# Weight splitting shared with GpSimd, the second token half first, and a new order of the stages

## The chip, the core and the metric

The program runs on one core of a Trainium2 chip, in one launch. The metric is the device time of that launch in microseconds (us): the median of three runs of the kernel before is 595.39 us (595.06 to 596.19). The profiled execution took 595.32 us, of which the span from the first to the last instruction in the trace is 593.5 us.

The engines are named as in the profile: PE is TensorE (its weight loads are PEld), DVE is VectorE, ACT is ScalarE, POOL is GpSimd, SP starts the transfers.

## What is computed

Two stages follow each other for each of 8 batches. The first is attention with 8 heads of 64 columns: 512 local tokens see a window of 32 tokens to each side and 32 global tokens; the 32 global tokens see all. The second is a gated layer over the 544 tokens of the batch.

```
s_l = softmax(0.125 * [q_l k_g^T, q_l k_l^T masked to |i-j| <= 32]);   out_l = s_l [v_g, v_l]
s_g = softmax(0.125 * q_g [k_g, k_l]^T);                               out_g = s_g [v_g, v_l]
x   = concat(out_g, out_l) as [batch, 544, 512]
h   = max(x @ w_in, 0)                       # 512 -> 1024
gate = sigmoid(conv_w[0]*h[t-1] + conv_w[1]*h[t] + conv_w[2]*h[t+1])
out = (h * gate) @ w_out                     # 1024 -> 512
```

The weights (w_in, w_out, conv_w) arrive as 64 bit floating point numbers, handed over as pairs of 32 bit words, and everything else as 32 bit. Both large products are made from two rounded parts of each operand: high times high, high times low, low times high. So each weight has to be turned from its two words into a high part (w0 below) and a low part before the first product that needs it.

## The kernel before

**Tiling.** A batch's attention goes by pairs of heads; a pair takes one load of queries and keys (`qk`), one of values (`vf`), 32 small score products into two banks (`ps_s`, key S), the softmax of each head (DVE finds the maximum and adds the mask, key M, line 285; ACT takes the exponential, key E, line 295), four transposes a head (`ps_t`, T), a copy (`a`, A), 32 small products with the values (`ps_v`, P), a division (`n`, N) and four transposes back (`pv`, U). Its result is rounded into `xh` (ACT) and the rest into `xl` (DVE, line 364), in two halves of the tokens, which overlap by two. The global tokens go by groups of four heads (keys G, GM, GE, GT, GC, GP, GO, GQ, GX), and end in the first 32 columns of the first half.

The gated layer goes by half batches of 272 tokens, `hh` = 0 to 15, and by eighths of the 1024 columns, so that `u` = 8 hh + ft counts 128 units. A unit is 12 products into one bank (`ps_h`, key PZ, line 460), a rectification (ACT, RE), the three taps (C1, Ca, Cb), and by pairs of units a tanh (ACT), the product with h (DVE, GG, line 498), its rounding (ACT, GH) and the rest (GL, line 215). Then come 4 output groups of 24 products (`ps_o`, keys Oa and Ob of 12 each, line 523), a copy (OE) and a store.

**The weights.** w_in and w_out come in four eighths each of 128 x 1024 numbers (index i = 0 to 3 for w_in, 4 to 7 for w_out). For each: a load of 1 MB (WD), the magnitude of the upper word (WA, ACT, line 112), clamp, shift and sign (WC, three DVE operations, lines 119, 120, 123), rounding to the high part (WH, ACT, line 212), and the low part (WL, four DVE operations, lines 126, 130, 132, 134). There is one buffer `wt` for it (`SLOTS["wt"]` = 1), so the next WA waits until the last reader of `wt` is done. Unit u needs eighth ft // 2 of w_in, and output group mt needs eighth 4 + mt.

**The order.** Nothing is left to a scheduler at run time. `plan` lists every step with its engine, an estimated duration (`cost`), what it waits for and a position, `arranged` plays this list through, taking on each engine the ready step with the lowest position, and `emit` writes the instructions in the order that comes out and ties each engine to it. So the tables `POS0` (first batch), `POS` (later batches), `LATE` and `WPOS` (the weights) decide which step stands in front of which on each engine, and each engine runs strictly in that order. `SHARED` names the DVE steps that the planner does not let run beside a POOL step.

In the first batch (`ENG0`) POOL does C1 and GL; in the later ones (`ENG`) C1 alone.

Of the kernel before, what the change touches and what calls it, by code (L numbers as in the profile page):

```python
# [52 lines left out]
def attn_moe(ctx: ExitStack, tc: tile.TileContext, qk_d, vw_d, qg_d, w_in_d, w_out_d, cw_d, out_d):  # L53
# [61 lines left out]

    def scaled_bits(w1, t, keep):

        v = nc.vector
        v.tensor_scalar(out=f(t), in0=f(t), scalar1=LEAST, scalar2=MOST, op0=ALU.max, op1=ALU.min)
        v.tensor_scalar(  # L120
            out=t, in0=t, scalar1=3, scalar2=0x3F800000 | keep, op0=ALU.logical_shift_left, op1=ALU.bitwise_and
        )
        v.scalar_tensor_tensor(out=t, in0=w1, scalar=0xC0000000, in1=t, op0=ALU.bitwise_and, op1=ALU.bitwise_or)  # L123
# [4 lines left out]
    def rest(on, out, w0, w1, p, low):  # L128

        nc.vector.tensor_scalar(out=w1, in0=w1, scalar1=low, scalar2=None, op0=ALU.bitwise_and)  # L130
# [1 line left out]
        v.scalar_tensor_tensor(out=f(w1), in0=w0, scalar=2.0**-32, in1=w1, op0=ALU.mult, op1=ALU.add)  # L132
        if on == "v":
            v.scalar_tensor_tensor(out=out, in0=f(w1), scalar=2.0**-20, in1=f(p), op0=ALU.mult, op1=ALU.mult)
# [61 lines left out]
    def WL(i):  # L196
# [3 lines left out]
        else:  # L200
# [720 lines left out]
```

## Time and profile before

| What | Value |
|---|---|
| median of 3 runs | 595.39 us |
| profiled execution, and its span | 595.32 us, 593.5 us |
| PE busy | 560.9 us, 95% of the span |
| DVE, ACT, POOL busy | 424.0, 324.2, 101.1 us (71%, 55%, 17%) |
| mean granted clock of TensorE | 0.982 |
| chain of work that ended last | PE 84%, DVE 9%, ACT 2% |
| output products (line 523) | 1536, mean 290 ns |
| hidden products (line 460) | 1024 + 512, mean 298 and 292 ns |
| the tap on POOL (line 248) | 128, mean 629 ns |
| the low part on POOL (line 215) | 8, mean 1484 ns |

Busy shares are means over the whole span; the 40 slices of the page and the windows of the trace show where an engine is full. The matmuls overlap each other, so a row's mean is longer than the step from one to the next: 12 of them take 1.52 us in the chain.

### The profile page before, as it was taken

Reading aid. Unit: us, or ns where it says so; the run is one execution under the profiler, and the core shown is the slowest. Engines: PE = TensorE matmul, PEld = TensorE weight load, DVE = VectorE, ACT = ScalarE, POOL = GpSimd, SP = SyncE. Lnnn points to the kernel's source line nnn. Section 1 sums busy time; section 2 is a strip of 40 time slices with the busy share of each in tenths; the row PEclk is TensorE's granted clock in tenths of the full one; section 3 lists DMA queues with packets and bytes.
Section 4 is the critical chain, followed back from the end, with each engine's and each line's share of the span. In section 5 each row is a group of like instructions: output and inputs, shape, how many; then the busy total and the mean of one; then the engine's idle time right before and its main releaser. Section 6 shows DMA issues by size and latency. Waiting matters only on the chain.

```text
span 593.5 us, 20757 instructions
## 1 busy us (share of the span) xinstructions
PE 560.9 (95%) x8704; PEld 528.8 (89%) x8704; DVE 424.0 (71%) x1388; ACT 324.2 (55%) x994; POOL 101.1 (17%) x190
## 2 busy tenths in 40 slices
PE   5656997999999999999999999999999999999997
PEld 3345896999999999999999999999999999999997
DVE  4999999689477948577685858668584856565651
ACT  4954794676477666446565655555565543333320
POOL 6000242033012111121111012111101212221210
PEclk9977999899999999999999999999999999999999
DMA  6987334156234332123333222232412000000001
GB/s 254 390 286 313 95 118 170 39 204 223 91 135 153 107 134 98 56 110 108 135 108 145 100 78 94 100 144 97 146 63 75 20 22 20 29 20 29 30 29 47
DMA packets 22125, 68.46 MB, mean 115 GB/s; under 512 B 2576, under 2 KB 12816, under 8 KB 21008
## 3 DMA queue, kind: packets, MB, share of 16 engines
q1 hardware_dynamic: 22032, 67.14, 31.2%
q8 instruction: 68, 1.11, 0.8%
q14 instruction: 25, 0.20, 0.1%
HBM read 58.22 MB, written 8.91 MB: 113 GB/s over the span
## 4 chain that ended last, share of the span: by engine, by line
PE 84%; DVE 9%; ACT 2%; issue 1%; DMA 1%; POOL 0%; DVEq 0%
PE ps_o L523 32%; PE ps_h L460 31%; PE ps_v L325 5%; PE ps_s L264 4%; PE ps_t L304 4%; PE pv L341 2%; PE psg L278 2%; PE go L422 2%; PE gt L406 1%; DVE pr L285 1%; DVE t L484 1%; DMA vf<-vw 1%; DVE wt L123 1%; DVE raw L132 1%; ACT pr L295 1%
## 5 line engine op out<-in xcount | busy, mean ns | idle before, releaser
L460 PE MATMUL ps_h<-xh,w_in 128*128 128x274 f32 x1024 | 225.4, 298 | 2.8 <-DVE raw L132 1.3
L523 PE MATMUL ps_o<-g,w_out 128*128 128x272 f32 x1536 | 212.2, 290 | 0.0
L523 PEld LDWEIGHTS ps_o<-g,w_out 128*128 128x128 f32 x1536 | 200.0, 189 | 0.2
L460 PEld LDWEIGHTS ps_h<-xh,w_in 128*128 128x128 f32 x1024 | 171.9, 191 | 6.3 <-ACT g L212 1.4
L248 POOL TENSOR_SCALAR t<-hb,cw 128x272 f32<-128x272 f32 x128 | 79.9, 629 | 425.7 <-ACT hb L469 159.2
L460 PE MATMUL ps_h<-xl,w_in 128*128 128x274 f32 x512 | 149.5, 292 | 0.8 <-issue 0.8
L484 DVE SCALAR_TENSOR_TENSOR t<-hb,cw,t 128x272 f32<-128x272 f32 x256 | 125.7, 514 | 30.5 <-POOL t L248 29.1
L295 ACT ACTIVATE pr<-pr,negm 128x128 f32<-128x128 f32 x256 | 99.5, 391 | 47.7 <-DVE negm L285 47.7
L469 ACT ACTIVATE hb<-ps_h 128x273 f32<-128x273 f32 x128 | 50.8, 398 | 93.4 <-PE ps_h L460 91.9
L460 PEld LDWEIGHTS ps_h<-xl,w_in 128*128 128x128 f32 x512 | 98.1, 192 | 1.0 <-issue 1.0
L285 DVE CUSTOM_DVE_ANT_0 pr<-ps_s,mask 128x128 f32<-128x128 f32 x256 | 57.8, 285 | 25.6 <-PE ps_s L264 23.2
L212 DVE COPY o<-ps_o 128x272 f32<-128x272 f32 x64 | 28.0, 438 | 54.8 <-PE ps_o L523 54.6
L212 ACT CAST g<-t 128x544 fp32r<-128x544 f32 x64 | 40.9, 646 | 34.5 <-DVE t L498 22.6
L498 DVE SCALAR_TENSOR_TENSOR t<-t,hb 128x544 f32<-128x544 f32 x64 | 46.0, 719 | 14.3 <-ACT t L493 13.3
L493 ACT ACTIVATE t<-t 128x544 f32<-128x544 f32 x64 | 42.4, 663 | 15.0 <-DVE t L484 13.9
L212 ACT COPY a<-ps_t 128x512 f32<-128x512 f32 x64 | 37.0, 583 | 23.2 <-PE ps_t L304 23.0
L295 ACT ACTIVATION_READ_ACCUMULATOR pr<-pr,negm 128x1 f32 x256 | 48.3, 189 | 0.0
L264 PE MATMUL ps_s<-qk 64*32 64x128 f32 x2048 | 38.4, 283 | 8.4 <-DMA qk<-qk 5.8
L304 PE MATMUL ps_t<-ident,pr 128*128 128x128 f32 x256 | 43.0, 282 | 3.5 <-ACT pr L295 2.5
L215 DVE TENSOR_TENSOR g<-t,g 128x544 fp32r<-128x544 f32 x56 | 41.0, 737 | 6.8 <-ACT g L212 5.3
L264 PEld LDWEIGHTS ps_s<-qk 64*32 64x32 f32 x2048 | 29.9, 109 | 12.7 <-DMA qk<-qk 5.8
L304 PEld LDWEIGHTS ps_t<-ident,pr 128*128 128x128 f32 x256 | 31.1, 144 | 8.2 <-ACT pr L295 7.6
(70 smaller groups left out, 466.1 us busy)
## 6 DMA issues: line engine op xcount, KB each, us to landing
vf<-vw SPq DMA_DIRECT2D x32, 896.0 KB, 6.3
qk<-qk SPq DMA_DIRECT2D x32, 592.0 KB, 4.9
out<-o SPq DMA_DIRECT2D x64, 136.0 KB, 1.7
raw<-w_in SPq DMA_DIRECT2D x4, 1024.0 KB, 6.6
raw<-w_out SPq DMA_DIRECT2D x4, 1024.0 KB, 6.6
qgf<-qg SPq DMA_DIRECT2D x16, 64.0 KB, 2.0
cwr<-cw SPq DMA_DIRECT2D x1, 24.0 KB, 1.9
```

Of the source, the lines that this page charges most:

```text
L212: nc.scalar.copy(out=out, in_=in_) if choice(key) == "a" else eng(key).tensor_copy(out=out, in_=in_)
L248: nc.gpsimd.tensor_scalar(out=out, in0=in_, scalar1=by, scalar2=0.0, op0=ALU.mult, op1=ALU.add)
L264: nc.tensor.matmul(heads[n + j]["s"][b * SG : (b + 1) * SG, t, :], lhsT=qk[rows, i * SG : (i + 1) * SG], rhs=qk[rows, a : a + P], start=Tr ...
L285: nc.vector.tensor_tensor_reduce(out=pr[:, t, :], in0=st["s"][:, t, :], in1=mask[:, t].rearrange("p a c -> p (a c)"), op0=ALU.add, op1=ALU ...
L295: nc.scalar.activation(out=st["p"][:, t, :], in_=st["p"][:, t, :], func=AF.Exp, scale=-1.0, bias=st["m"][:, t : t + 1], accum_out=two["r"] ...
L304: nc.tensor.transpose(out=st["t"][:, t, :], in_=st["p"][:, t, :], identity=ident)
L460: nc.tensor.matmul(ps, lhsT=w[:, ft, ct, :], rhs=x, start=i == 0, stop=i == 3 * NCT - 1)
L469: nc.scalar.activation(out=o, in_=z, func=AF.Relu, scale=0.5)
L484: nc.vector.scalar_tensor_tensor(out=st["t"], in0=st["h"][:, k : k + HALF], scalar=cw[:, 3 * ft + k : 3 * ft + k + 1], in1=st["t"], op0=AL ...
L493: nc.scalar.activation(out=t, in_=t, func=AF.Tanh)
L498: nc.vector.scalar_tensor_tensor(out=t, in0=t, scalar=1.0, in1=h, op0=ALU.add, op1=ALU.mult)
L523: nc.tensor.matmul(ps, lhsT=w[:, mt, ft, :], rhs=g[:, ft, :], start=ft + i == 0, stop=ft == NFT - 1 and i == 2)
```

## The change

- For each eighth of the weights the clamp (a step of its own now, WM, line 117) goes from DVE to POOL. DVE keeps shift and sign (WC, lines 122 and 125).
- The low part is made in another way. WC keeps more bits in `wt`. WL is two DVE operations that do not need the high part: the power of two of the number (line 128) and its product with the lower word (line 214). Two new steps on POOL take the difference of `wt` and the high part (WS, line 221) and add that product (WT, line 226). WT is what the products now wait for. `wt` comes free after WS.
- `TURN` = 1: of each batch the second half of the tokens goes through the gated layer first, so that the first units no longer wait for the global tokens.
- In the first batch C1 goes from POOL to ACT.
- 17 instead of 13 pairs of x buffers; all tables of positions, and some of the planner's durations, are new. `SHARED` loses Ca, Cb, GG, GL and WL.

How many products PE does, and their shapes, stay as they were, 1536 for `ps_h` and 1536 for `ps_o` among them.

The order of the instructions shows three places.

**DVE at the start.** First the kernel before, from the end of the tap weights on: `pr,negm` is M (with a row for its second instruction), `ps_s` the scores.

```order
L132 SCALAR_TENSOR_TENSOR cwr<-cwr 128x24
L134 SCALAR_TENSOR_TENSOR cwp<-cwr,cwp 128x24
L159 TENSOR_TENSOR cw<-cw,cwp 128x24
L285 ISA pr,negm<-ps_s,mask 128x128
L285 ISA negm 128x1
```

Then the change at the same place, with what each waits for:

```order
L135 SCALAR_TENSOR_TENSOR cwp<-cwr,cwp 128x24 [waits DVE_49]
L158 TENSOR_TENSOR cw<-cw,cwp 128x24 [waits DVE_49]
L122 TENSOR_SCALAR wt<-wt 128x1024 [waits Pool_49]
L125 SCALAR_TENSOR_TENSOR wt<-raw,wt 128x1024 [waits DMAHW1_49,DVE_49]
L308 ISA pr,negm<-ps_s,mask 128x128 [waits PE_49]
L308 ISA negm 128x1
```

The first M of the program now stands behind WC of the first eighth, which waits for POOL.

**POOL after its masks.** `wt`, `raw` and `w_in` are the weights, `g` and `t` GL of the first batch. The kernel before has only C1 and GL here; the change has

```order
L117 TENSOR_SCALAR wt<-wt 128x1024
L221 TENSOR_TENSOR w_in_152<-wt,w_in_151 128x1024
L226 TENSOR_TENSOR w_in_152<-w_in_152,raw 128x1024
L117 TENSOR_SCALAR wt<-wt 128x1024
L238 TENSOR_TENSOR g_1169<-t,g_1168 128x544 x2
L221 TENSOR_TENSOR w_out_154<-wt,w_out_153 128x1024
L226 TENSOR_TENSOR w_out_154<-w_out_154,raw 128x1024
L238 TENSOR_TENSOR g_1169<-t,g_1168 128x544
```

the first three rows once for each of four eighths of w_in, then the four of w_out with four GL in between; the other four GL come behind the last eighth.

**SP at the start.** `qk` are queries and keys, `raw` the weights. Before:

```order
L149 DMA cwr<-cw 128x48
L242 DMA qgf<-qg 128x128 x2
L229 DMA qk<-qk 128x1184 x2
L174 DMA raw<-w_in 128x2048
L229 DMA qk<-qk 128x1184
```

and with the change:

```order
L147 DMA cwr<-cw 128x48
L173 DMA raw<-w_in 128x2048
L265 DMA qgf<-qg 128x128 x2
L252 DMA qk<-qk 128x1184 x3
L173 DMA raw<-w_in 128x2048 x2
```

The first eighth of the weights is loaded in front of the first queries and keys.

The core of the diff:

```diff
+    def clamp(e, t):
+        e.tensor_scalar(out=f(t), in0=f(t), scalar1=LEAST, scalar2=MOST, op0=ALU.max, op1=ALU.min)
+
     def scaled_bits(w1, t, keep):
         v = nc.vector
-        v.tensor_scalar(out=f(t), in0=f(t), scalar1=LEAST, scalar2=MOST, op0=ALU.max, op1=ALU.min)
         v.tensor_scalar(
             out=t, in0=t, scalar1=3, scalar2=0x3F800000 | keep, op0=ALU.logical_shift_left, op1=ALU.bitwise_and
         )
...
+    def WM(i):
+        if wpe == 2:
+            clamp(nc.gpsimd, wf[i])
+
     def WC(i):
         if wpe == 2:
-            scaled_bits(raw[i][:, :, 1], wf[i], 0x7FF000)
+            if WAY[i] != "q":
+                clamp(nc.vector, wf[i])
+            scaled_bits(raw[i][:, :, 1], wf[i], 0x7FF000 if WAY[i] == "v" else 0x7FFFF8)
...
-        else:
+        elif WAY[i] == "v":
             p = wf[i]
             power(p, p)
-            rest(choice("WL"), lo, raw[i][:, :, 0], raw[i][:, :, 1], p, 0x1FF)
+            rest(lo, raw[i][:, :, 0], raw[i][:, :, 1], p, 0x1FF)
+        else:
+            w0, p = raw[i][:, :, 0], raw[i][:, :, 1]
+            power(p, wf[i])
+            nc.vector.scalar_tensor_tensor(
+                out=f(w0), in0=w0, scalar=2.0**-52, in1=f(p), op0=ALU.mult, op1=ALU.mult
+            )
+
+    def WS(i):
+        hi, lo = parts(i)
+        if wpe == 2:
+            nc.gpsimd.tensor_tensor(out=lo, in0=f(wf[i]), in1=f(hi), op=ALU.subtract)
+
+    def WX(i):
+        hi, lo = parts(i)
+        if wpe == 2:
+            nc.gpsimd.tensor_tensor(out=lo, in0=f(lo), in1=f(raw[i][:, :, 0]), op=ALU.add)
...
+    def half_of(hh):
+        return (hh + TURN) % 2
+
     def Z(u):
         hh, ft = divmod(u, NFT)
-        b, half = divmod(hh, 2)
+        b, half = hh // 2, half_of(hh)
...
 SLOTS = dict(
-    ps=8, x=13, hb=2, qk=3, vf=3, qg=2, p=4, r=3, a=4, n=2, pg=1, pgt=1, t=2, o=2, wt=1, g0=2, g1=2,
+    ps=8, x=17, hb=2, qk=3, vf=3, qg=2, p=4, r=3, a=4, n=2, pg=1, pgt=1, t=2, o=2, wt=1, g0=2, g1=2,
 )
...
 ENG0 = dict(
-    A="a", GC="a", XH="a", GX="v", RE="a", C1="p", GH="a", GL="p", OE="v", WA="a", WH="a", WL="v",
+    A="a", GC="a", XH="a", GX="v", RE="a", C1="a", GH="a", GL="p", OE="v", WA="a", WH="a",
 )
 POS = dict(
-    LQ=-3.56, LG=-53.13, LV=12.71, S=-3.9, M=7.61, E=46.84, NS=-11.03, T=-16.54, A=-39.33, P=-1.74, N=0.2, U=-7.02,
+    LQ=-32.96, LG=-84.61, LV=4.16, S=-7.39, M=21.65, E=51.87, NS=23.31, T=-25.66, A=-28.74, P=-21.63, N=17.3,
...
-WPOS = [11.57, -8.05, 1.24, 15.47, 1.38, 33.08, 13.87, 67.5]
+WPOS = [13.36, -73.44, -6.93, 28.88, 52.69, 58.02, 74.3, 68.57]
+TURN = 1
+WAY = "qqqqqqqq"
...
-SHARED = ("C1", "Ca", "Cb", "GG", "GH", "GL", "WC", "WH", "WL")
+SHARED = ("C1", "GH", "WC", "WH")
...
+        if WAY[i] == "q":
+            op("WM", i, t + POS0["WM"], 0, [("WA", i)], [], ["wt%d" % i])
...
+            op("WL", i, t + POS0["WL"], 0, [("WC", i)], [], ["raw%d" % i, "wt%d" % i])
+            op("WS", i, t + POS0["WS"], 0, [("WH", i)], [], ["wt%d" % i])
+            op("WT", i, t + POS0["WT"], 0, [("WS", i), ("WL", i)], [], ["raw%d" % i])
...
-            ready += [("GX", 8 * b + 3), ("GX", 8 * b + 7)] * (half == 0) + [("WL", ft // 2)]
+            ready += [("GX", 8 * b + 3), ("GX", 8 * b + 7)] * (half == 0) + [weight(ft // 2)]
```

More of the change, by code (lines that the diff above doesn't have):

```diff
@@ L155, in attn_moe @@
         magnitude(w1, t)
+        clamp(nc.vector, t)
         scaled_bits(w1, t, 0x7FFFF8)
         power(cwp, t)
-        rest("v", f(cwp), w0, w1, cwp, 0)
+        rest(f(cwp), w0, w1, cwp, 0)
         nc.vector.tensor_tensor(out=cw, in0=cw, in1=f(cwp), op=ALU.add)
@@ L463, in RE @@
     def RE(u):
-        half = u // NFT % 2
+        half = half_of(u // NFT)
         o = hid[u]["h"][:, 1 - half : HW - half]
@@ L495, in GG @@
     def GG(u):
-        t, half = hid[u]["two"], u // NFT % 2
+        t, half = hid[u]["two"], half_of(u // NFT)
         h = hb[u // 2 % SLOTS["hb"]][:, :, half + 1 : half + 1 + HALF]
@@ L528, in OE @@
         hh, mt = divmod(o, NCT)
-        b, half = divmod(hh, 2)
         t = outs[o] = moe.tile([P, HALF], F32, name="o", bufs=SLOTS["o"])
@@ L534, in ST @@
         hh, mt = divmod(o, NCT)
-        b, half = divmod(hh, 2)
+        b, half = hh // 2, half_of(hh)
         nc.sync.dma_start(out=out_d[b, mt, :, half * HALF : (half + 1) * HALF], in_=outs[o])
@@ L658, in op @@
         if names:
-            e = dict(p=PE, s=SP, a=ACT)[names[0]]
-            c = "v"
+            e = dict(p=PE, v=DVE, g=POOL, s=SP, a=ACT)[names[0]]
+            c = WAY[i] if key in ("WL", "WC") else "v"
         else:
@@ L706, in plan @@
             at_n("U", [("N", e)], [("ps", f"pv{p}")], [f"n{p}"], i=e)
+            last = "XY"[1 - TURN]
             for half, x in enumerate("XY"):
                 name = f"x{b},{h // 2},{half}"
-                at_n(x + "H", [("U", e)] + [("YH", e - 2)] * (e > 0), [("x", name)], [f"pv{p}"], i=e)
+                at_n(x + "H", [("U", e)] + [(last + "H", e - 2)] * (e > 0), [("x", name)], [f"pv{p}"], i=e)
                 at_n(x + "L", [(x + "H", e)], [], [f"pv{p}", name], i=e)
@@ L725, in plan, with weight @@
     return ops
+def weight(i):
+    return ("WL" if WAY[i] == "v" else "WT", i)
 def units(op, late, b):
@@ L730, in units @@
         hh = 2 * b + half
+        half = (half + TURN) % 2
         x = [f"x{b},{ct},{half}" for ct in range(NCT)]
@@ L758, in units @@
             g = [f"g0{hh}", f"g1{hh}"]
-            at_o("Oa", [("GL", 8 * hh + 1), ("GL", 8 * hh + 3), ("WL", 4 + mt)], [("ps", f"o{o}"), ("o_", f"o{o}o")], g)
+            at_o("Oa", [("GL", 8 * hh + 1), ("GL", 8 * hh + 3), weight(4 + mt)], [("ps", f"o{o}"), ("o_", f"o{o}o")], g)
             at_o("Ob", [("Oa", o), ("GL", 8 * hh + 5), ("GL", 8 * hh + 7)], [], [f"o{o}"] + g)
```

45 lines of the change are left out of this document (22 added, 23 removed).

## The prediction

> **What bounds the kernel now.** First the windows (columns: stretch and its length; busy us of PE, PEld, DVE, ACT, POOL; granted clock, DMA share, GB/s), then PE's waits (us in total, times, longest).
>
> ```profile
> 0.00:110.00 110.00, 82.14 (x1689) 68.15 (x1690) 95.24 (x318) 69.89 (x215) 23.89 (x70) 0.91 0.59 221
> 110.00:560.00 450.00, 448.43 (x6777) 430.59 (x6776) 316.25 (x1046) 248.78 (x770) 74.87 (x116) 1.00 0.27 95
> 53.57:104.30 50.73, 44.92 (x827) 39.39 (x826) 49.80 (x162) 34.40 (x110) 13.91 (x15) 0.93 0.37 133
> 104.30:110.00 5.70, 5.70 (x37) 5.70 (x34) 1.81 (x12) 1.87 (x4) 0.49 (x1) 0.70 0.09 27
> PE pv L341 <- DVE n L333: 7.5, 4, 5.5
> PE ps_s L264 <- DMA qk<-qk: 5.8, 1, 5.8
> ```
>
> From 110 to 560 us PE lacks 1.6 us of 450, at full clock, and DVE has 30% to spare. Before 110 PE lacks 27.9 us and its clock is 0.91; there DVE is the full engine (49.80 of 50.73 us from 53.57 to 104.3). So batches 1 to 7 can give nothing, and the question is by how much earlier PE becomes full for good. Three moments on PE:
>
> ```profile
> 5.81 3.67 PE L264 MATMUL ps_s<-qk 64*32 64x128 f32 x128 [5.81 <-DMA qk<-qk]
> 53.57 0.37 PE L460 MATMUL ps_h<-xh,w_in 128*128 128x274 f32 x1
> 129.49 3.25 PE L523 MATMUL ps_o<-g,w_out 128*128 128x272 f32 x24
> ```
>
> The first hidden product stands at 53.57. The third row serves as a mark: behind it (131.5 to 132.6; I take 132.6, where its step ends) before has done what the change, by its order, has done ahead of the first product with the last eighth of w_out. Both have 11 score pairs, 10 P and 10 U; the change has 18 instead of 17 units, 22 instead of 20 T, one G, GP and GQ more, and 6 instead of 9 half output groups. The three half groups (1.51 us each by 21.20 us for 168 products, last row of PE, so 4.5 us) pay for the unit (1.5 us) and the rest (some 3 us). The time at which the change gets there, against 132.6, is the gain.
>
> ```profile
> 569.12 21.20 PE L523 MATMUL ps_o<-g,w_out 128*128 128x272 f32 x168
> ```
>
> **What DVE is relieved of.** The weight operations (mean ns, 7 of 8 eighths; L134 in its larger group):
>
> ```profile
> L119 DVE TENSOR_SCALAR wt<-wt 128x1024 f32<-128x1024 f32 x7 | 4.7, 673 | 0.2 <-ACT wt L112 0.2
> L120 DVE TENSOR_SCALAR wt<-wt 128x1024 uint32<-128x1024 uint32 x7 | 5.0, 720 | 0.2
> L123 DVE SCALAR_TENSOR_TENSOR wt<-raw,wt 128x1024 uint32<-128x1024 uint32 x7 | 9.6, 1373 | 0.2
> L126 DVE TENSOR_SCALAR wt<-wt 128x1024 uint32<-128x1024 uint32 x7 | 4.8, 685 | 0.0
> L130 DVE TENSOR_SCALAR raw<-raw 128x1024 uint32<-128x1024 uint32 x7 | 4.9, 694 | 0.0
> L132 DVE SCALAR_TENSOR_TENSOR raw<-raw 128x1024 f32<-128x1024 uint32 x7 | 8.9, 1266 | 0.2
> L134 DVE SCALAR_TENSOR_TENSOR w_in<-raw,wt 128x1024 fp32r<-128x1024 f32 x4 | 4.9, 1226 | 0.1
> ```
>
> Together 6.64 us an eighth. The change keeps two like L120 and L126 and two like L123 and L132: 4.0 us with these means, 3.9 with L123 undisturbed. DVE gets back 2.7 us an eighth, 21 us in all.
>
> **What POOL gets.** The trace has no POOL operation of 1024 columns. The nearest rows, and a copy of 32 columns for what a call costs by itself:
>
> ```profile
> 154.99 0.49 POOL L248 TENSOR_SCALAR t<-hb,cw 128x272 f32<-128x272 f32 x1 [8.97 <-ACT hb L469]
> 140.04 1.36 POOL L215 TENSOR_TENSOR g<-t,g 128x544 fp32r<-128x544 f32 x1 [1.51 <-ACT g L212]
> L105 POOL COPY mask<-corner 32x32 f32<-32x32 f32 x30 | 5.4, 203 | 0.7
> ```
>
> In proportion to the columns the clamp takes 1.84 us and a two-input operation 2.56; with 0.2 us of each being fixed, 1.29 and 2.38. I take 1.5 and 2.4, nearer the lower end, since a fixed part is there: 6.3 us an eighth (6.0 to 7.0), 50 us for all, none of it on PE's path by itself. But POOL and DVE get in each other's way:
>
> ```profile
> 140.63 0.79 DVE L377 TENSOR_TENSOR gnegm<-gnegm 128x1 f32<-128x1 f32 x1
> 87.08 1.80 POOL L215 TENSOR_TENSOR g<-t,g 128x544 fp32r<-128x544 f32 x1 [6.94 <-ACT g L212]
> 87.70 2.26 DVE L123 SCALAR_TENSOR_TENSOR wt<-raw,wt 128x1024 uint32<-128x1024 uint32 x1
> ```
>
> A one-column DVE operation that began at 140.63 ended when POOL's did (140.04 + 1.36 = 141.40). At 87.08 POOL took 1.80 us, the 0.44 more being what was left of DVE's operation then, and L123 took 1.0 more than its usual 1.23. So I count a POOL operation and a DVE operation with two inputs from SBUF, or with one and the fast copy of L119's kind, as using one thing in turn. The Trainium skill, page "SBUF — State Buffer", section "SBUF: two separate sides", has this as a rule: a port pair shared by the two, locked for the whole instruction. The three rows agree with it. It speaks against this change: moving elementwise work from DVE to POOL then frees DVE only for what reads PSUM.
>
> **The start.**
>
> ```profile
> 11.01 0.21 POOL L105 COPY mask<-corner 32x32 f32<-32x32 f32 x1
> 11.25 0.29 DVE L285 CUSTOM_DVE_ANT_0 pr<-ps_s,mask 128x128 f32<-128x128 f32 x1 [1.31 <-POOL mask L105]
> ```
>
> POOL is busy with masks to 11.22. The first clamp follows (to 12.7), then WC on DVE (1.95 us, to 14.8), and only then M, which ACT's exponentials need. The load of 1 MB in front of the queries (at about 300 GB/s 3.4 us, so scores from 9.2 instead of 5.81) is hidden by this wait. Up to the high part of the third eighth ACT has, from 14.8:
>
> ```profile
> 16.83 1.54 ACT pr L295 x8
> L112 ACT ACTIVATE wt<-raw 128x1024 f32<-128x1024 f32 x5 | 5.8, 1165 | 6.8 <-DVE w_in L134 3.6 <-DVE w_out L134 3.2
> L212 ACT COPY a<-ps_t 128x512 f32<-128x512 f32 x8 | 4.4, 576 | 0.0
> L212 ACT CAST w_in<-wt 128x1024 fp32r<-128x1024 f32 x3 | 3.1, 1041 | 0.7 <-DVE wt L123 0.7
> L212 ACT CAST xh<-pv 128x274 fp32r<-128x274 f32 (+1 forms) x8 | 2.6, 377 | 1.5 <-PE pv L341 1.5
> L212 ACT COPY pgt<-gt 96x512 f32<-96x512 f32 (+2 forms) x6 | 2.0, 365 | 0.0
> L382 ACT ACTIVATE pg<-pg,gnegm 128x544 f32<-128x544 f32 x2 | 1.5, 746 | 0.3 <-DVE gnegm L377 0.3
> ```
>
> Eight heads of exponentials 12.3, two WA 2.3, three WH 3.1, eight copies 4.6, four xh 1.5, three pgt 1.1, two global ones 1.5: 26.4, so 41.2, and with 1.5 for waits 42.7. WS and WT on POOL follow (4.8): the third eighth is ready at 47.5, and PE, which has a GQ and a score pair ahead, starts the hidden products at 48, 5.5 us earlier than 53.57. That the second half goes first saves nothing here: GQ still stands ahead on PE.
>
> **From 48 to the last eighth.** What uses the shared thing from 47.5: five eighths at 6.3 + 3.9 = 51.0. Of the gated layer, Ca, Cb and GG of the seven pairs that must be through (with two `hb` buffers unit 16, which stands ahead of the mark, needs pair 6):
>
> ```profile
> 62.93 1.74 DVE L484 SCALAR_TENSOR_TENSOR t<-hb,cw,t 128x272 f32<-128x272 f32 x4
> L498 DVE SCALAR_TENSOR_TENSOR t<-t,hb 128x544 f32<-128x544 f32 x5 | 3.6, 716 | 0.0
> ```
>
> 2.4 us a pair (the second row overlaps its neighbour by 0.06), 16.8; four GL, 5.4; the attention's small sums some 3. In all 76.2: fully packed it ends at 123.7. It isn't: `wt` has one buffer, so per eighth WA and WH (2.2 us on ACT) interrupt the chain; half of that is filled by other work, 1.1 x 5 = 5.5. So 129.2, and PE, ready earlier, waits for it: 132.6 - 129.2 = 3.4 us gained. Ends: 123.7 (gain 8.9) and, with the whole 2.2 and POOL's upper prices (5 x 0.7), 138.2 (loss 5.6).
>
> Taken at nothing: C1 on ACT (16 x 0.40, under ACT's 34.40 of 50.73); the new tables for later batches, since PE waits 1.6 us there and DVE, ACT and POOL have 30% and more free as cover (gone, a few us); buffers of x. The last output group and its store end as before.
>
> Sum: 595.32 - 3.4 = 591.9; the median lies 0.07 above the profiled execution, so 592.0.
>
> **The rivals.** *The relief counts in full* (0.17): POOL's operations fall where DVE reads PSUM, as M, N and xl do, and PE is held by nothing after 48. From 53.57 to 132.6 before needs 79 us, with 5.8 of waits and, by clock 0.93 and 0.70, 4.8 of lost clock in it; without them, and with a G and T done before 48 (1.4): 48 + 67 = 115, gain 17.6, 578. For it: POOL used only 13.91 of 50.73 us. Against it: most DVE rows there are of the blocked kind. Between that and the forecast lies what I count here, 578 to 586.
>
> *The shared thing takes more than DVE is relieved of* (0.25): the last eighth comes after 133.8. From there on it costs; at 138.2 it is 595.4 + 5.6 = 601.0, and PE's clock may suffer from its own waits:
>
> ```profile
> 43.55 1.97 PE L341 MATMUL pv<-ident,n 128*128 128x128 f32 x8 [5.49 <-DVE n L333]
> 40.00:50.00 10.00, 4.96 (x126) 4.37 (x129) 9.80 (x18) 4.38 (x9) 0.00 (x0) 0.66 0.89 340
> 50.00:60.00 10.00, 6.82 (x114) 4.60 (x96) 9.69 (x27) 4.00 (x11) 1.05 (x1) 0.69 0.62 232
> ```
>
> After 5.49 us without work the clock was 0.66 and 0.69 for 20 us: two such waits with a third of 5 us of work each lost are 3 us, and 604 is the end. I name 600, halfway between 596.6 and 604. For it: to stay under 133.8 the shared thing must be used 88% of the time (76.2 of 86.3 us), by engines that run strictly in order, and DVE stands still behind POOL's operations.
>
> *No change that can be measured* (0.16): gain and loss within 1.2 us, 594.2 to 596.6.
>
> **How the numbers follow.** The forecast, a gain of 1.2 to 9 us (586 to 594.2), has 0.42, and it is 592.0. About 0.2% (1.2 us) is what a measurement of this kernel tells from no change. Faster 0.42 + 0.17 = 0.59, same 0.16, slower 0.25. The range for 8 in 10 runs from 583 (part of the full relief) to 600 (the middle of the slower case).
>
> **What will show it.** Right: M starts near 15 us; the first `ps_h` near 48; POOL near 60% busy from 48 to 129, with weight operations of 1.5 and 2.4 us and DVE rows of L125, L214 and L510 lengthened by up to 2.4; PE's waits from 60 to 130 on GG and WT; the last WT near 129; a full PE from there. Wrong: a `ps_h` row much later than 48 (ACT's sum), a last WT before 120 or after 137 (the packing), or waits of PE of more than 3 us in all after 150 (the tables).

## The result, and the profile after

The change makes the kernel slower: 606.33 us median (605.78 to 606.53, 4 runs) against 595.79 us (595.06 to 597.51, 4 runs) before, a ratio of 1.0171 (95% interval 1.0147 to 1.0195). The profiled execution took 606.26 us, with a span of 604.5 us, 11.0 us more than before.

First the windows of the changed kernel, with the columns of those shown before:

```profile
0.00:110.00 110.00, 76.29 (x1572) 62.19 (x1573) 88.27 (x269) 70.33 (x218) 65.42 (x75) 0.89 0.59 217
110.00:560.00 450.00, 444.72 (x6808) 427.19 (x6807) 318.81 (x1058) 251.33 (x775) 80.62 (x115) 1.00 0.28 96
150.00:560.00 410.00, 410.00 (x6155) 395.68 (x6154) 281.00 (x944) 223.34 (x685) 58.58 (x106) 1.00 0.26 90
```

Before 110 us PE now lacks 33.7 us instead of 27.9, and up to 560 another 5.3 instead of 1.6; all of the 5.3 lies before 150 us. POOL is at 65.42 us instead of 23.89. What it does with that stands in the groups of POOL (mean ns after the busy time):

```profile
L117 POOL TENSOR_SCALAR wt<-wt 128x1024 f32<-128x1024 f32 x8 | 29.2, 3654 | 7.5 <-ACT wt L112 7.4
L221 POOL TENSOR_TENSOR w_out<-wt,w_out 128x1024 fp32r<-128x1024 f32 x4 | 9.7, 2433 | 8.0 <-DVE negm L308 4.8 <-ACT w_out L235 3.2
L226 POOL TENSOR_TENSOR w_in<-w_in,raw 128x1024 fp32r<-128x1024 f32 x4 | 9.7, 2414 | 2.6 <-issue 2.4
```

Difference and sum cost the 2.4 us that were expected. The clamp costs 3.65 us, where I had taken 1.5 (ends 1.29 and 1.84); on DVE it took 0.67. DVE's groups of the first 150 us:

```profile
L510 DVE SCALAR_TENSOR_TENSOR t<-hb,cw,t 128x272 f32<-128x272 f32 x28 | 22.7, 830 | 0.7 <-ACT t L269 0.6
L214 DVE SCALAR_TENSOR_TENSOR raw<-raw 128x1024 f32<-128x1024 uint32 x8 | 16.1, 2010 | 0.3
L338 DVE TENSOR_SCALAR sums<-sums 128x8 f32<-128x8 f32 x11 | 10.6, 959 | 0.3 <-ACT pr L318 0.3
L128 DVE TENSOR_SCALAR raw<-wt 128x1024 uint32<-128x1024 uint32 x8 | 7.7, 962 | 0.0
L524 DVE SCALAR_TENSOR_TENSOR t<-t,hb 128x544 f32<-128x544 f32 x6 | 6.5, 1089 | 0.0
L122 DVE TENSOR_SCALAR wt<-wt 128x1024 uint32<-128x1024 uint32 x8 | 5.5, 690 | 14.7 <-POOL wt L117 14.7
L415 DVE TENSOR_SCALAR gw<-whose,gsum 128x2 f32<-128x2 f32 x6 | 3.1, 521 | 0.2
```

The same kinds of rows in the kernel before, for the same stretch:

```profile
L484 DVE SCALAR_TENSOR_TENSOR t<-hb,cw,t 128x272 f32<-128x272 f32 x38 | 17.3, 501 | 3.5 <-POOL t L248 3.5
L132 DVE SCALAR_TENSOR_TENSOR raw<-raw 128x1024 f32<-128x1024 uint32 x8 | 10.1, 1261 | 0.3
L315 DVE TENSOR_SCALAR sums<-sums 128x8 f32<-128x8 f32 x12 | 2.2, 182 | 0.3 <-ACT pr L295 0.3
L392 DVE TENSOR_SCALAR gw<-whose,gsum 128x2 f32<-128x2 f32 x6 | 1.6, 259 | 0.2
```

With 0.69 and 0.72 us as the usual lengths of L128 and L524 (L126 and L498 in the rows of before), DVE's rows are longer by 28 x 0.33 + 8 x 0.75 + 11 x 0.78 + 8 x 0.27 + 6 x 0.37 + 6 x 0.26 = 30 us. On top of that DVE waits 14.7 us for clamps. It was relieved of some 21 us of work and lost some 44. The most telling row is L338: eight columns of sums, 0.18 us of work, took 0.96 us on average. How that looks in time (start, duration):

```profile
63.08 3.36 POOL L221 TENSOR_TENSOR w_in<-wt,w_in 128x1024 fp32r<-128x1024 f32 x1 [3.21 <-DMA qk<-qk]
66.51 2.46 POOL L226 TENSOR_TENSOR w_in<-w_in,raw 128x1024 fp32r<-128x1024 f32 x1
...
64.10 2.63 DVE L510 SCALAR_TENSOR_TENSOR t<-hb,cw,t 128x272 f32<-128x272 f32 x1
66.66 2.35 DVE L338 TENSOR_SCALAR sums<-sums 128x8 f32<-128x8 f32 x1
```

In 4.9 us DVE got through one tap and one set of small sums. The tap ended 0.3 us after the difference did (63.08 + 3.36 = 66.44), the small sums when POOL's sum did, near 69. Nothing behind them on DVE could start before, not even what reads PSUM. The first hidden product, and then the end of it:

```profile
58.48 0.39 PE L486 MATMUL ps_h<-xh,w_in 128*128 128x274 f32 x1
136.88 2.39 POOL L221 TENSOR_TENSOR w_out<-wt,w_out 128x1024 fp32r<-128x1024 f32 x1 [4.80 <-DVE negm L308]
137.01 2.82 DVE L128 TENSOR_SCALAR raw<-wt 128x1024 uint32<-128x1024 uint32 x1
141.23 2.39 POOL L226 TENSOR_TENSOR w_out<-w_out,raw 128x1024 fp32r<-128x1024 f32 x1 [1.95 <-issue]
142.59 0.66 PE L364 MATMUL pv<-ident,n 128*128 128x128 f32 x4 [1.62 <-DVE n L356]
145.60 1.75 PE L549 MATMUL ps_o<-g,w_out 128*128 128x272 f32 x12
```

The first hidden product starts at 58.48 (53.57 before), and the last eighth is ready at 143.6 instead of the predicted 129.2. PE does not wait for it: its last wait before it stays full ends at 142.59 and is for a division on DVE (N), and what PE has in front of the first product with the last eighth takes it to 145.60. Both come late by the same thing. L128 of the last eighth, 0.69 us of work, took 2.82 us beside POOL's difference, and behind it on DVE stood the product that the last sum needs (L214) and that N.

### The profile page after: what moved, and what is told of

Read it like the earlier page. It is cut to its first block, busy times and chain, and to the rows that moved or that the text cites. A ratio compares the mean times of both kernels' runs of the same rounds, so it can differ in the third digit from the quotient of the medians.

```text
span 604.5 us, 20797 instructions
## 1 busy us (share of the span) xinstructions
PE 562.3 (93%) x8704; PEld 530.4 (88%) x8704; DVE 426.6 (71%) x1364; ACT 331.4 (55%) x1010; POOL 150.1 (25%) x198
## 4 chain that ended last, share of the span: by engine, by line
PE 77%; DVE 13%; POOL 5%; ACT 3%; issue 2%; POOLq 0%; DVEq 0%
PE ps_o L549 31%; PE ps_h L486 29%; PE ps_v L348 4%; PE ps_s L287 3%; PE ps_t L327 3%; POOL wt L117 3%; DVE t L510 2%; PE pv L364 2%; DVE raw L214 2%; PE psg L301 2%; DVE sums L338 1%; DVE wt L125 1%; PE go L445 1%; PE gt L429 1%; DVE raw L128 1%
## 5 line engine op out<-in xcount | busy, mean ns | idle before, releaser
L549 PE MATMUL ps_o<-g,w_out 128*128 128x272 f32 x1536 | 214.6, 290 | 0.0
L510 DVE SCALAR_TENSOR_TENSOR t<-hb,cw,t 128x272 f32<-128x272 f32 x256 | 136.6, 538 | 54.1 <-POOL t L271 51.4
L271 POOL TENSOR_SCALAR t<-hb,cw 128x272 f32<-128x272 f32 x112 | 59.9, 535 | 368.6 <-ACT hb L495 347.0
L524 DVE SCALAR_TENSOR_TENSOR t<-t,hb 128x544 f32<-128x544 f32 x64 | 48.9, 765 | 45.2 <-ACT t L519 45.1
L308 DVE CUSTOM_DVE_ANT_0 pr<-ps_s,mask 128x128 f32<-128x128 f32 x256 | 56.5, 283 | 0.1
L327 PE MATMUL ps_t<-ident,pr 128*128 128x128 f32 x256 | 42.2, 287 | 13.0 <-ACT pr L318 10.2
L235 DVE COPY o<-ps_o 128x272 f32<-128x272 f32 x64 | 27.9, 436 | 24.4 <-PE ps_o L549 24.4
L287 PE MATMUL ps_s<-qk 64*32 64x128 f32 x2048 | 36.4, 286 | 8.9 <-DMA qk<-qk 8.9
## 6 DMA issues: line engine op xcount, KB each, us to landing
qk<-qk SPq DMA_DIRECT2D x32, 592.0 KB, 5.3
```

Source lines behind the costliest of these rows:

```text
L235: nc.scalar.copy(out=out, in_=in_) if choice(key) == "a" else eng(key).tensor_copy(out=out, in_=in_)
L271: nc.gpsimd.tensor_scalar(out=out, in0=in_, scalar1=by, scalar2=0.0, op0=ALU.mult, op1=ALU.add)
L287: nc.tensor.matmul(heads[n + j]["s"][b * SG : (b + 1) * SG, t, :], lhsT=qk[rows, i * SG : (i + 1) * SG], rhs=qk[rows, a : a + P], start=Tr ...
L308: nc.vector.tensor_tensor_reduce(out=pr[:, t, :], in0=st["s"][:, t, :], in1=mask[:, t].rearrange("p a c -> p (a c)"), op0=ALU.add, op1=ALU ...
L327: nc.tensor.transpose(out=st["t"][:, t, :], in_=st["p"][:, t, :], identity=ident)
L510: nc.vector.scalar_tensor_tensor(out=st["t"], in0=st["h"][:, k : k + HALF], scalar=cw[:, 3 * ft + k : 3 * ft + k + 1], in1=st["t"], op0=AL ...
```

## The experiments

Three theories were on trial. A: the clamp's price on POOL is the loss. B: POOL's operations with two inputs make DVE stand still, which eats what DVE is relieved of. C: the new order, the second half first and C1 on ACT cost it. All ratios are against the kernel before, on the same chip.

**The clamp back on DVE.** In the changed kernel:

```diff
 def WM(i):
-    clamp(nc.gpsimd, wf[i])
+    pass
 def WC(i):
-    if WAY[i] != "q":
-        clamp(nc.vector, wf[i])
+    clamp(nc.vector, wf[i])
```

> The clamp goes back to DVE, as the first instruction of WC; every instruction keeps its place in the order of each engine, only POOL has eight fewer. The clamp took 3.65 us on POOL and 0.67 on DVE, where it was priced at 1.5 on POOL. Theory A (the clamp's price on POOL is the loss: WA, WM, WC, WH and WS follow each other through one buffer, so eight times some 2.1 us come on top of the forecast): the chain gets 2.95 us shorter per eighth; the third eighth is ready near 45 (52.9 with the change), the last near 123 to 129 (143.6), and the time is 586 to 593. Rival B (POOL's difference and sum, which shut DVE out for 2.4 us each, already eat what DVE is relieved of): the last eighth stays after 136, 599 to 605. Rival C (the new order, the second half first, C1 on ACT): nothing of it is undone here, so the time stays above 600 although the last eighth comes early.

601.04 us, ratio 1.0093 (1.0074 to 1.0112). So 5.3 of the 10.5 us come back. A's 586 to 593 is missed, B's 599 to 605 met; C's time of over 600 is met too. DVE waits for no clamp any more, but its rows beside difference and sum stay long (0 to 150 us):

```profile
L212 DVE SCALAR_TENSOR_TENSOR raw<-raw 128x1024 f32<-128x1024 uint32 x8 | 14.0, 1756 | 0.3
L128 DVE TENSOR_SCALAR raw<-wt 128x1024 uint32<-128x1024 uint32 x8 | 10.5, 1314 | 0.0
L336 DVE TENSOR_SCALAR sums<-sums 128x8 f32<-128x8 f32 x11 | 9.8, 889 | 0.3 <-ACT pr L316 0.3
```

The last eighth is ready late as well, which B and not C had expected (row of the timeline):

```profile
136.03 2.39 POOL L224 TENSOR_TENSOR w_out<-w_out,raw 128x1024 fp32r<-128x1024 f32 x1 [1.95 <-issue]
```

**Another operation in the clamp's place.** In the changed kernel, at the same place on POOL:

```diff
 def WM(i):
-    clamp(nc.gpsimd, wf[i])
+    nc.gpsimd.tensor_scalar(out=f(wf[i]), in0=f(wf[i]), scalar1=1.0, scalar2=0.0, op0=ALU.mult, op1=ALU.add)
```

> The clamp on POOL is replaced by a multiplication by 1.0 and an addition of 0.0 over the same 128x1024 numbers, in the same place of the order: the clamp's effect on extreme weights is left out, nothing else. The tap on POOL is of this kind (0.49 us for 272 columns), so by columns 1.3 to 1.84 us each, against 3.65 for the clamp. Theory A: with the price that the prediction used, the prediction's result comes out: last eighth near 129 (at most 133), 591 to 595. Rival B: as A only in the price of the row, but the time stays at 599 or more. Rival C: 600 or more with the last eighth early. Should a 1024-column operation of any kind take 3.6 us on POOL (a price by size, not by the maximum and minimum), the time stays at 606.

597.81 us, ratio 1.0032 (1.0016 to 1.0049), between A's 591 to 595 and B's 599. The group of the operation, and then the last sum in the timeline:

```profile
L190 POOL TENSOR_SCALAR wt<-wt 128x1024 f32<-128x1024 f32 x8 | 8.6, 1079 | 8.1 <-ACT wt L112 8.0
```

```profile
133.67 2.40 POOL L226 TENSOR_TENSOR w_out<-w_out,raw 128x1024 fp32r<-128x1024 f32 x1 [1.95 <-issue]
```

It takes 1.08 us, less even than the 1.5 that I had priced, and 8.5 us come back. But the last eighth is ready at 136.1, not 129.2, and the time is not 592. So the price of the clamp is the larger part of the loss, and something else keeps the forecast from coming true even with a cheaper operation.

**What one-input operations cost on POOL.** Each eighth got another form in the clamp's place:

```diff
 def WM(i):
-    clamp(nc.gpsimd, wf[i])
+    one of: max | min | mult | mult, max | max, add | copy | clamp in four pieces | clamp
```

> A measurement of POOL prices, one form for each of the eight eighths in place of the clamp, each over 128x1024 numbers: maximum alone; minimum alone; multiplication alone; multiplication and maximum; maximum and addition; copy; the clamp in four pieces of 256 columns; the clamp. All but the last two leave out a part of the clamp or all of it. Theory A, price by operation: the forms without a maximum or minimum take 1.3 to 1.84 us, each maximum or minimum adds about 1 us, so 2.5 for one and 3.6 for two; the four pieces together 3.6 plus three times 0.2. If it is the size of the instruction: all single forms near 3.6 and the four pieces clearly less. If two constants cost: the one-operation forms half of the others.

The groups of POOL in that run, in the order maximum, minimum, multiplication, multiplication and maximum, maximum and addition, copy, pieces, clamp:

```profile
L191 POOL TENSOR_SCALAR wt<-wt 128x1024 f32<-128x1024 f32 x1 | 2.8, 2788 | 0.0
L193 POOL TENSOR_SCALAR wt<-wt 128x1024 f32<-128x1024 f32 x1 | 2.8, 2781 | 0.1
L195 POOL TENSOR_SCALAR wt<-wt 128x1024 f32<-128x1024 f32 x1 | 2.8, 2779 | 0.5 <-ACT wt L112 0.5
L197 POOL TENSOR_SCALAR wt<-wt 128x1024 f32<-128x1024 f32 x1 | 3.6, 3636 | 3.3 <-ACT wt L112 3.3
L199 POOL TENSOR_SCALAR wt<-wt 128x1024 f32<-128x1024 f32 x1 | 3.6, 3636 | 0.0
L201 POOL COPY wt<-wt 128x1024 f32<-128x1024 f32 x1 | 1.3, 1335 | 1.2 <-ACT wt L112 1.2
L205 POOL TENSOR_SCALAR wt<-wt 128x256 f32<-128x256 f32 x4 | 4.6, 1183 | 2.4 <-ACT wt L112 2.4
L207 POOL TENSOR_SCALAR wt<-wt 128x1024 f32<-128x1024 f32 x1 | 3.6, 3616 | 0.0
```

None of the expectations holds in full. A multiplication alone costs as much as a maximum alone, 2.78 us; two operations cost 3.62 to 3.64 in the three pairs of this run, but 1.08 as multiplication and addition (the run before this one). Why that pair is cheap no run shows. The tap on POOL, from which I had scaled the clamp, is this one cheap pair. The Trainium skill, page "GPSIMD Engine Reference", section "3.1 Elementwise — side-by-side cycle accounting", gives 1.03 cycles an element for up to two operations. At the clock of 1.2 GHz that the page states (section "1. Specifications") an estimate from it is 0.88 us for 1024 elements. The rows agree only for that pair (1.08) and roughly for the copy (1.34), not for the other forms of 1024 columns (2.78 to 3.64).

**The order with all weight work on DVE, arranged anew.** The changed kernel with

```diff
-WAY = "qqqqqqqq"
+WAY = "vvvvvvvv"
```

> All weight work goes back to DVE (the way of the kernel before: seven DVE operations an eighth), and the steps are arranged anew by the changed tables; the second half first, C1 of the first batch on ACT and the buffers of x stay. These tables have no entry made for this. Rival C: what is left of the change still costs, 600 or more, and PE lacks some 5 us between 150 and 560. Theory A: the rest of the change does nothing of size: 592 to 600, DVE the full engine up to about 130, and PE lacks less than 5 us from 150 on. Rival B: as A.

599.89 us, ratio 1.0075 (1.0055 to 1.0095), inside A and B, at their upper end, and not clear of C's 600. PE lacks nothing from 150 to 560 us, so C's sign is not there; but since the tables were not made for these steps, the run says little about what the order is worth. The kernels with a fixed order, below, settle that.

**Each part alone.** First the weight part in the kernel before, whose order is otherwise kept:

```diff
-        v.tensor_scalar(out=f(t), in0=f(t), scalar1=LEAST, scalar2=MOST, op0=ALU.max, op1=ALU.min)
+        nc.gpsimd.tensor_scalar(out=f(t), in0=f(t), scalar1=LEAST, scalar2=MOST, op0=ALU.max, op1=ALU.min)
...
-            power(p, p)
-            rest(choice("WL"), lo, raw[i][:, :, 0], raw[i][:, :, 1], p, 0x1FF)
+            power(p, wf[i])        # p: the upper words' buffer, w0: the lower words
+            nc.vector.scalar_tensor_tensor(out=f(w0), in0=w0, scalar=2.0**-52, in1=f(p), op0=ALU.mult, op1=ALU.mult)
+            nc.gpsimd.tensor_tensor(out=lo, in0=f(wf[i]), in1=f(hi), op=ALU.subtract)
+            nc.gpsimd.tensor_tensor(out=lo, in0=f(lo), in1=f(w0), op=ALU.add)
```

> The kernel before, with its own order, tables, halves and C1; only the weight work is changed, at the places where it stands there: the clamp on POOL, shift, sign, power and product on DVE, difference and sum on POOL. Theories A and B: 600 to 612, since each eighth has 3.65 us of clamp for which DVE now waits (3 us more than it took itself), and its low part comes some 2.8 us later (1.97 us on DVE and 4.8 on POOL against 3.87). Theory C: the weight part is harmless in an order that suits, 591 to 597.

617.75 us, ratio 1.0383 (1.0351 to 1.0414), slower than any expectation. DVE's wait for the clamp (the number behind the second bar) is the largest of all runs:

```profile
L120 DVE TENSOR_SCALAR wt<-wt 128x1024 uint32<-128x1024 uint32 x8 | 5.5, 692 | 18.8 <-POOL wt L119 18.8
```

The same without the first pair of lines, so with the clamp left on DVE:

> The kernel before in its own order, with POOL's difference and sum in place of the last two of DVE's weight operations and the clamp left on DVE. DVE is relieved of 2.0 us an eighth, 15.6 us in all. Theory A alone (only the clamp's price was wrong): 588 to 595. Theory B: what DVE is relieved of comes back as standing still (26 us in the run with the clamp on DVE), and the low parts come some 2.8 us later: 596 to 604.

603.13 us, ratio 1.0135 (1.0109 to 1.0161): within B's 596 to 604, out of A's. Here difference and sum alone, which take 15.6 us from DVE, cost 7.6 us. And the rest of the change alone, with the weight work and the position tables of the kernel before, in short:

```diff
-ENG0: C1="p"      SLOTS: x=13      first half first
+ENG0: C1="a"      SLOTS: x=17      TURN = 1
```

> The other part alone: weight work as in the kernel before, all on DVE, the old tables of positions, but the second half of the tokens first, C1 of the first batch on ACT and 17 pairs of x buffers. Theories A and B: nothing of size, 592 to 599, as these tables were not made for it. Theory C: 600 or more, PE lacking more than 5 us behind 150 us.

596.55 us, ratio 1.0018 (1.0004 to 1.0032), as A and B expected. So halves, C1 and buffers cost nothing of size; of C that leaves the new tables, which the runs with all weight work on DVE in the changed order, below, put to the test.

**Without difference and sum.** The run with the clamp on DVE, and

```diff
 def WL(i):
-    nc.vector.scalar_tensor_tensor(out=f(w0), in0=w0, scalar=2.0**-52, in1=f(p), ...)
+    nc.vector.scalar_tensor_tensor(out=lo, in0=w0, scalar=2.0**-52, in1=f(p), ...)
 def WS(i), WX(i):
-    nc.gpsimd.tensor_tensor(...)
+    pass
```

> As the run with the clamp on DVE, but POOL's difference and sum are left out as well, so that POOL has no weight work at all: the product of power and lower word is written straight into the low part, which is then only a share of what the reference needs. DVE has the same instructions in the same order as in that run (601.0), where its rows for the first 150 us were some 26 us longer than without POOL beside them (small sums 889 ns against 182, the power 1314 against 685, the product with the lower word 1756 against 1261, taps 628 against 501). Theory B, now beside A (while POOL holds the thing that both use, DVE stands still with all that is queued behind): these rows go back to 0.18, 0.69, 1.25 and 0.50 us, the last eighth comes before 122, and the time is 582 to 590. Theory C (the order itself): PE's waits stay, 597 or more.

577.97 us, ratio 0.9721 (0.9681 to 0.9761), below B's 582 to 590. Its rows answer to those of the run with the clamp on DVE:

```profile
L212 DVE SCALAR_TENSOR_TENSOR w_out<-raw 128x1024 fp32r<-128x1024 uint32 x4 | 4.9, 1226 | 0.1
L128 DVE TENSOR_SCALAR raw<-wt 128x1024 uint32<-128x1024 uint32 x8 | 5.5, 689 | 0.0
L334 DVE TENSOR_SCALAR sums<-sums 128x8 f32<-128x8 f32 x13 | 2.2, 166 | 1.7 <-ACT pr L314 1.6
```

These are back at their own lengths. POOL's two operations cost 23 us in this order. But two things went at once: the standing still, and the 4.8 us by which each low part comes later and each buffer is held longer.

**One input in place of two.** To part these, POOL got two operations as long as difference and sum, with the same waits and buffers:

```diff
 def WS(i):
-    nc.gpsimd.tensor_tensor(out=lo, in0=f(wf[i]), in1=f(hi), op=ALU.subtract)
+    nc.gpsimd.tensor_scalar(out=lo, in0=f(wf[i]), scalar1=-BIG, scalar2=None, op0=ALU.max)
 def WX(i):
-    nc.gpsimd.tensor_tensor(out=lo, in0=f(lo), in1=f(raw[i][:, :, 0]), op=ALU.add)
+    nc.gpsimd.tensor_scalar(out=lo, in0=f(raw[i][:, :, 0]), scalar1=-BIG, scalar2=None, op0=ALU.max)
```

> As the run without difference and sum (578.0), in its order, but with two POOL operations of one input in their places and with their waits: the maximum of the number and -3e38 into the low part, then the maximum of the product and -3e38 over it, 2.78 us each by the measured prices (difference and sum took 2.4). The low part is the same share as there; the difference is left out again. POOL is busy longer than with difference and sum, the low part is ready later than there, and it waits for and holds the same buffers; only the second input is gone. Theory B in its narrow form (it is the second input of POOL's operation that shuts DVE out): DVE's rows keep their lengths (0.17 for the small sums, 0.69 for the power, 1.25 for the product), and the time is 578 to 588. If it is the lateness of the low part or the held buffers, or if every POOL operation of this size shuts DVE out: 598 or more, in the first case with DVE's rows short, in the second with them long.

583.59 us, ratio 0.9799 (0.9783 to 0.9815), inside the 578 to 588 of B's narrow form. (One wait differs: the first operation no longer reads the high part, so it may start 1.04 us earlier, which its length makes up.) First groups of 0 to 150 us, then the start in time:

```profile
L219 POOL TENSOR_SCALAR w_in<-wt 128x1024 fp32r<-128x1024 f32 x4 | 11.9, 2966 | 19.2 <-DVE wt L125 14.0 <-DVE gsum L410 5.1
L212 DVE SCALAR_TENSOR_TENSOR raw<-raw 128x1024 f32<-128x1024 uint32 x8 | 10.5, 1317 | 0.3
L336 DVE TENSOR_SCALAR sums<-sums 128x8 f32<-128x8 f32 x13 | 3.4, 261 | 1.6 <-ACT pr L316 1.6
```

```profile
13.13 2.77 POOL L219 TENSOR_SCALAR w_in<-wt 128x1024 fp32r<-128x1024 f32 x1
13.29 1.43 DVE L128 TENSOR_SCALAR raw<-wt 128x1024 uint32<-128x1024 uint32 x1
14.75 1.23 DVE L212 SCALAR_TENSOR_TENSOR raw<-raw 128x1024 f32<-128x1024 uint32 x1
```

POOL is busy longer than in the run at 601.0, and each low part still waits for two POOL operations, yet DVE's rows are much nearer to their own lengths. L128 lost 0.7 us, and did not wait for POOL's end at 15.90; L212, with two inputs, lost nothing beside it. Added up over the rows that grew (L128 with 900 ns against 689 and the taps with 663 against 591 among them), DVE's work in the first 150 us is some 9 us longer than with no weight work on POOL, against some 24 with difference and sum. So of the 23 us some 17 went with the second input, or with the kind of instruction, which changed together with it. The remaining 5.6 belong to lateness, held buffers and the rest of the standing still, which this run does not part.

The rest of the standing still has a form: a one-input operation held DVE in its first microsecond or so, and the small sums also near its end. In the changed kernel sums that began 1.1 us into a clamp (at 25.73, the clamp at 24.62) took 0.16 us, while sums that began 0.93 us before the end of one ended with it:

```profile
37.76 3.63 POOL L117 TENSOR_SCALAR wt<-wt 128x1024 f32<-128x1024 f32 x1
40.46 0.96 DVE L338 TENSOR_SCALAR sums<-sums 128x8 f32<-128x8 f32 x1
```

The Trainium skill, page "SBUF — State Buffer", section "Who interferes with whom", lets a DVE instruction with two SBUF inputs contend with any GpSimd instruction that reads SBUF, for the whole instruction. For POOL operations with two inputs the rows agree; for this form with one input they do not, as L212 ran at its own length beside it.

**Difference and sum on DVE.** The run with the clamp on DVE, with `nc.gpsimd` turned into `nc.vector` in WS and WX.

> As the run with the clamp on DVE (601.0), in its order, but difference and sum go to DVE as well, at the places where POOL's stood in time: all eight weight operations (7.1 us an eighth) are on DVE, and POOL has none. DVE gets 2.46 us an eighth, 19.7 us in all; for that the 26 us by which its rows were longer beside POOL go. Theory B: POOL's two operations cost DVE more than doing them itself: 592 to 599. If POOL did relieve DVE, and the loss lay elsewhere: 606 to 615, by the 19.7 us of work added to the full engine.

592.81 us, ratio 0.9958 (0.9938 to 0.9979), inside B's 592 to 599. This is the plainest verdict on the change's idea:

```profile
L219 DVE TENSOR_TENSOR w_out<-wt,w_out 128x1024 fp32r<-128x1024 f32 x4 | 4.9, 1219 | 0.0
L224 DVE TENSOR_TENSOR w_out<-w_out,raw 128x1024 fp32r<-128x1024 f32 x4 | 4.9, 1224 | 0.0
L336 DVE TENSOR_SCALAR sums<-sums 128x8 f32<-128x8 f32 x12 | 2.0, 163 | 0.0
```

DVE does each in 1.22 us; on POOL each shut DVE out for up to 2.4. Giving the full engine 19.7 us more work made the kernel 8 us faster than the run with only the clamp back on DVE.

**The old arithmetic in the new order.** The changed kernel with the clamp in WC, no WM, WS and WX, and

```diff
 def WL(i):
+    v.tensor_scalar(out=w1, in0=w1, scalar1=0x1FF, scalar2=None, op0=ALU.bitwise_and)
+    v.scalar_tensor_tensor(out=f(w1), in0=w0, scalar=2.0**-32, in1=w1, op0=ALU.mult, op1=ALU.add)
+    power(w0, wf[i])
+    v.scalar_tensor_tensor(out=lo, in0=f(w1), scalar=2.0**-20, in1=f(w0), op0=ALU.mult, op1=ALU.mult)
```

> The changed kernel's order, but with the weight arithmetic of the kernel before, all on DVE at the places of WC and WL (the power goes into the buffer of the lower word, so that the low part need not wait for the high part): 6.64 us an eighth instead of 7.06 with difference and sum on DVE (592.8), 3.4 us less in all on the full engine, and the low part ready without the two steps behind it. Theory B (what counts is DVE's own time plus its standing still, in this order): 587 to 591. If the order itself were worse than the one before: 595 or more.

592.16 us, ratio 0.9949 (0.9932 to 0.9965), a little above what was expected: the 3.4 us less on DVE gave 0.6. But it shows what the order (with halves, C1, buffers and a low part that no longer waits for the high part) is worth by itself: 3 us less than before, so the new tables cost nothing either and C is out. With this the loss can be laid out in one order, step by step: 592.2 with all on DVE in the old way, 592.8 in the new way, 601.0 with difference and sum on POOL (+8.2), 606.3 with the clamp there too (+5.3).

**A version from what was learnt.** The old arithmetic on DVE as in the run before, the clamp of the third to the seventh eighth on POOL with its measured price and a place where no wait of DVE for it shows, first half first, C1 of the first batch on ACT, and tables searched anew with these prices in the planner:

```diff
-WAY = "qqqqqqqq"
+WAY = "vvcccccv"      # c: clamp on POOL, the rest on DVE
-WM=(1480, 1560)
+WM=(3640, 3670)
-TURN = 1
+TURN = 0
```

> A version made from what the runs showed: weight arithmetic of the kernel before on DVE, but the clamp of five of the eight eighths on POOL with its measured price of 3.64 us and placed where its lateness is covered (one input, so it should not shut DVE out); first half first; C1 of the first batch on ACT; the steps arranged anew with these prices. Nothing is left out. Theory B: DVE is relieved of five times 0.67 us, 3.4 us, and C1 no longer holds POOL beside DVE: 586 to 593. If a long one-input operation shuts DVE out as well, or the clamp lies in the chain as in the change: 596 to 605.

588.56 us, ratio 0.9879 (0.9847 to 0.9911), inside the 586 to 593 expected and faster than both kernels. A window, and the group of the clamp on POOL:

```profile
0.00:110.00 110.00, 88.54 (x2078) 72.76 (x2079) 98.49 (x378) 88.91 (x291) 34.94 (x63) 0.95 0.71 264
```

```profile
L117 POOL TENSOR_SCALAR wt<-wt 128x1024 f32<-128x1024 f32 x5 | 18.1, 3624 | 47.0 <-ACT wt L112 47.0
```

PE lacks 21.5 us before 110 instead of 27.9. The small sums took 259 ns there, against 164 in the run before, so the clamps still held DVE up a little. Since tables, places and the clamps were changed together, how much each gave was not tried.

## Why the prediction was wrong, point by point

Three steps of it failed. The clamp was priced at 1.5 us on POOL and took 3.65. The shared work was packed as if DVE went on with other work beside POOL, and DVE stood still. And the wait on which the sum is built, PE's for the last eighth, is not in the trace.

**Which stretch decides** was right: from 150 to 560 us PE waits for nothing (1.6 us before), and the loss lies in front of that. The yardstick gave the right number, but not for the reason stated. 143.6 less the 132.6 of the mark is 11.0 us, and the span grew by 11.0; with the clamp on DVE (138.4) and with the cheap operation (136.1) it holds within 0.1 us too. But from 60 to 130 us PE waits for N (5.0 us), an exponential (2.9), a copy of the output (2.2) and the global tokens (1.3), not for GG and WT as predicted, and its last wait, to 142.59, is for N again. From the end of that wait to the end of the span it is 461.9 us, and in those two runs 461.9 and 462.1. The last eighth and that N came late by the same L128. In the run with the old arithmetic on DVE the last eighth was ready at 126.4, which by the yardstick makes a span of 587.3; PE's wait for N ended at 127.88, and the span was 590.4, 462.5 us behind it. So it was luck in part that the yardstick held.

**The price of POOL's clamp** is the term that failed most. "I take 1.5" was scaled by columns from a row of the same engine and kind, but of another pair of operations; measured 3.65, twice the upper end of 1.84. Replaced by an operation of 1.08, the time fell by 8.5 us. Not all of the price came through: eight times 2.57 us are 20.6, and the last eighth came 7.5 us later with them (143.6 against 136.1), since DVE and ACT did other work while POOL clamped.

**Two-input operations on POOL** (2.4) were right: 2.41 to 2.43 where undisturbed.

**What DVE is relieved of** was right as work, 2.7 us an eighth, but it never arrived. In the first 150 us DVE was busy for 126.07 us, of which some 30 were standing still, and it waited 14.7 us more for clamps.

**That POOL and DVE use one thing in turn** was right, and I weighed it: "moving elementwise work from DVE to POOL then frees DVE only for what reads PSUM". What failed is the packing, 76.2 us of shared work plus 5.5 of interruption. It let DVE's other work run beside POOL, and counted the small sums with some 3 us. But DVE works strictly in order: a small operation stuck behind POOL holds the PSUM work behind it too, and each of the eleven sums lost 0.78 us. With 1.08 us in the clamp's place, less than the 1.5 of the forecast, the last eighth should have been there before 129.2; it came at 136.1, and from the third eighth to the last it took 87.2 us instead of the 81.7 of the forecast. The run that left the second input away (583.6) and the one that gave the work back to DVE (592.8) show that this is the step that failed beside the price. Of the 14.3 us between 592.0 and 606.3, 8.5 lie between the clamp and the cheap operation, and 5.8 are left for this; the gain of the new order, not counted in the forecast, hides some of it.

**The start.** The third eighth was predicted for 47.5; with the cheaper operation it came at 46.47 + 2.39 = 48.9, with the clamp at 52.9, so ACT's sum was about right, with three operations 0.4 us cheaper each than priced. PE's hidden products, predicted right behind it at 48, began at 54.0 and 58.5: ahead of them on PE stood more global work than the GQ and one score pair that I had counted, and it was late itself. Its lateness is the standing still once more: in the same order, with the clamp on DVE, they began at 54.26 with difference and sum on POOL, at 46.84 without them and at 48.16 with the one-input operations. That the first M waits behind the first clamp was taken as harmless. It began at 16.8 instead of near 15, and PE's waits for ACT's exponentials rose from 2.5 us (four waits, the longest 1.1) to 10.2:

```profile
PE ps_t L327 <- ACT pr L318: 10.2, 3, 4.9
```

**Tables, C1, halves and buffers taken at nothing**: nearly right. The rest alone gave +1.0 us in the old order; the new order with all weight work on DVE gave 3 us less than before, a gain that I had not counted.

**The rivals.** "The shared thing takes more than DVE is relieved of" was the one, with 0.25, and its rule for the price (595.4 plus what the last eighth comes after 132.6) gives 606.4 for 143.6. Its end, 138.2, was too early, as POOL's upper price for the clamp (1.84) was half of the real one. "Full relief" at 578 is also the time of the run in which POOL had no weight work (578.0), but that agreement shows little: there the clamp is on DVE, and a part of the low parts is left out.

## What to carry to other kernels

Price an operation on POOL by a row of the same pair of operations, not of the same instruction: the cheap pair here took 1.08 us, its neighbours 2.78 to 3.65. Before work goes from DVE to POOL, ask whether POOL's operation has two SBUF inputs; if so, count its whole duration as DVE's, since DVE runs in order and even an eight-column operation waits for the end, and compare that with the time DVE would need itself. An engine that shows as full may be standing still: look at the mean of its smallest operations.

## What the runs showed of the hardware that I had not expected

- On POOL, a 128x1024 operation with constants takes 1.08 us as multiplication and addition, 2.78 as a maximum, a minimum or a multiplication alone, and 3.62 to 3.65 as each of the three other pairs that were tried; a copy takes 1.34.
- A two-input POOL operation of 2.4 us held DVE up far more (1756 ns against 1226 for the product with two inputs, 889 against 166 for the small sums) than a one-input one of 2.8 us (1317 and 261). In the run with one input, small sums that began 0.6 us into POOL's operation ended 1.2 us after its start (29.42 to 29.94, POOL's from 28.78), sums that began 1.1 us into one were not held (41.54 to 41.70, POOL's from 40.48 to 43.33), and sums that began 0.66 us before the end of one ended with it (121.38 to 122.07, POOL's from 119.12 to 122.04).
- Beside a two-input POOL operation, a DVE operation with one input and eight columns is held up as long as a large one: up to 2.37 us for 0.17 us of work.
